# A Fourier mix and a two-layer product on one core: an opening with another stage A and other weight order, and a chunk's block sums moved behind other work

## The chip, the cores and the metric

The kernel runs on one core of a Trainium2 chip. The time is that of the device for one execution, in microseconds (us). Five engines work beside each other and wait for each other through semaphores: TensorE (PE) multiplies matrices into PSUM, VectorE (DVE), ScalarE (ACT) and GpSimd (POOL) work on elements, and SyncE (SP) issues the transfers, which 16 DMA engines carry out between the device memory and the on-chip buffers.

## The reference

```python
# x: (8, 3008, 256); w_r, w_i: (256, 256); b_r, b_i: (256,)
X = np.fft.rfft(x, axis=1)                      # along the 3008 positions
Yr = Xr @ w_r - Xi @ w_i + b_r
Yi = Xr @ w_i + Xi @ w_r + b_i
Y  = sign(Y) * max(|Y| - 0.01, 0)               # for Yr and Yi each
y  = np.fft.irfft(Y, n=3008, axis=1)            # float32
# y as (24064, 256); w_in: (256, 2048); w_out: (2048, 256), both float64
h  = np.maximum(y @ w_in, 0.0)
out = (h * h @ w_out).astype(np.float32)
```

## The kernel before, in words

3008 = 47 x 64, and the transform is done in two factors. Position n is written with n1 (47 values) and n2 (64 values); of the 47 frequencies of the first factor only r = 0 to 23 are needed, since x is real.

- **Stage A** is the 47-point transform. The host has paired the rows n1 and 47 - n1 (`folded_rows`), 24 pairs for each n2, and lays five n2 side by side, so a tile has 120 rows (`GROUPS`: 12 of width 5 and one of 4, 96 rows). VectorE adds and subtracts the two halves (`fold`, L214 and L215), and two products with the table `tA` give `psa`. ScalarE copies it (`eva`) and a transfer stores it in a scratch area in device memory, `scr1[r, n2, ...]`, 24 outer rows (`store_a`, L207).
- **Stage B** goes over 12 pairs of frequencies r. Per pair it loads 128 rows (`bin`, `load_b`), does the 64-point transform (`points_b`, L223, tile `psb`), mixes with w_r and w_i (three real products instead of four, with the sum of both parts `sum_x` and with combined weights; `psm`), adds the bias (`add_e`), takes the threshold, turns the result (`zh`), does the 64-point inverse (`psc`) and stores `evc` in a second scratch area (`store_c`, L211).
- **The inverse** of the first factor loads 120 rows of it for five n2 (`din`, L251), multiplies (`points_d`, `psd`, L261), and unfolds (`dx`), and the result `xt`, split into a high and a low part, is the input of the second half. Two such groups, 470 positions, are a chunk; there are 52.
- **The two-layer product** takes a chunk in 8 rounds. In a round `mm1` makes 256 of the 2048 hidden rows (12 matmuls of 470 columns, `ph`), `squares` and `sums` make seven combinations `g` of them, which are split into `gh` and `gl`, and `mm2`, two rounds later, does 21 matmuls with the prepared weights `wo_` into four accumulators `po`. Products are exact to float32 by three matmuls with high and low parts (`mm3`, L186 to L188). When a chunk's last round is done, `put_together` makes the output from the four accumulators: a ScalarE copy and seven VectorE sums (L768 to L776).

The opening, `start()`, does stage A and stage B of batch 0, stage A of batch 1, the first chunk's inverse, and brings w_in and w_out in: they come as float64, 512 KB a piece, and `narrow` makes float32 of the bits. In the opening the products of stages A and B are plain float32 matmuls, and the order of instructions on the engines is left to a scheduler. The batches after that do the same stages inside the main rounds, on a plan written out by hand: `plan_a`, `plan_b` and `plan_d` put each step at a round and a place, and a round runs its places in this order: load, a1, `mm1`, p1, `squares`, v1, `sums`, `mm2`, p2, a2, `put_together` if a chunk ends here, v2. The letter says the engine: a ScalarE, v VectorE, p TensorE.

At v2 stand the low part of a stage A input (`fl`, L557), that of a stage B input (`xl`, L606), the adding of the bias and the unfolding `dx`; what uses them stands mostly in p1 of the next round. The small products take their PSUM from two buffers (`ps_f`) in turn.

Of the kernel before, what the change touches and what calls it, by code (L numbers as in the profile page):

```python
# [44 lines left out]
W = 5  # L45
# [34 lines left out]

def _cs(num, den):

    num = np.asarray(num) % den
    ang = 2.0 * np.pi * num / den
    c, s = np.cos(ang), np.sin(ang)
    c = np.where((4 * num) % (2 * den) == den, 0.0, c)
    s = np.where((2 * num) % den == 0, 0.0, s)
    return c, s


def tables():
# [39 lines left out]
    return dict(t_a=ta.astype(np.float32), t_b=tb.astype(np.float32), t_m=tm.astype(np.float32),  # L131
# [15 lines left out]
def fft_mix_moe(ctx: ExitStack, tc: tile.TileContext, xp, w_r, w_i, b_r, b_i,  # L147
                w_in, w_out, t_a, t_b, t_m, t_d, sgn, outT):
    nc = tc.nc
    B = xp.shape[0]  # L150
# [24 lines left out]
    wi_ = [ctile(f"wi{k}", [P, 2, DFF], F32R) for k in range(2)]  # L175
    wo_ = []

    def split(src, hi, lo):

        nc.scalar.copy(hi, src)  # L180
        nc.vector.tensor_sub(lo, src, hi.bitcast(F32))
# [16 lines left out]
    def load_x(b, i, t):  # L198
        nc.sync.dma_start(out=t, in_=xp[b].rearrange("g p d -> p g d")[:t.shape[0], i, :])
# [76 lines left out]
    def start():  # L276

        with ExitStack() as own:
            sb = own.enter_context(tc.tile_pool(name="sb0", bufs=2))
            pp = own.enter_context(tc.tile_pool(name="ps0", bufs=8, space=bass.MemoryType.PSUM))  # L280

            def tl(tag, shape=(P, 512), dt=F32, bufs=2, name=None):
                return sb.tile(list(shape), dt, tag=tag, name=name or tag, bufs=bufs)
# [4 lines left out]
            tA = tl("tA", (120, 4, 120), bufs=1)  # L288
            tM = tl("tM", (P, P), bufs=1)
            wmf = [tl(f"wmf{k}", (P, 3, D), bufs=1) for k in range(2)]  # L290

            def load_mix():
                nc.sync.dma_start(out=tB[:, :5], in_=t_b[:, :5])
                yield
                wr = tl("ld", bufs=4, name="wr").rearrange("p (k e) -> p k e", k=2)
                wi = tl("ld", bufs=4, name="wi").rearrange("p (k e) -> p k e", k=2)
                nc.sync.dma_start(out=wr, in_=w_r.rearrange("(k p) e -> p k e", p=P))
                nc.sync.dma_start(out=wi, in_=w_i.rearrange("(k p) e -> p k e", p=P))
                nc.sync.dma_start(out=bias2[:, 0, :], in_=b_r.partition_broadcast(P))
                nc.sync.dma_start(out=bias2[:, 1, :], in_=b_i.partition_broadcast(P))  # L300
                nc.sync.dma_start(out=sg, in_=sgn)
                nc.sync.dma_start(out=tM, in_=t_m)
                yield
                for k in range(2):
                    nc.scalar.copy(wmf[k][:, 0], wr[:, k])
                    nc.vector.scalar_tensor_tensor(wmf[k][:, 1], wr[:, k], -1.0, wi[:, k],
                                                   op0=ALU.mult, op1=ALU.subtract)
                    nc.vector.tensor_sub(wmf[k][:, 2], wi[:, k], wr[:, k])
                nc.sync.dma_start(out=tB[:, 5:], in_=t_b[:, 5:])
                nc.sync.dma_start(out=tD, in_=t_d)  # L310
                yield

            def narrow(t, h):
# [4 lines left out]
                nc.scalar.activation(h, hi.bitcast(F32), AF.Abs)  # L318
                nc.vector.tensor_scalar(h, h, F_MIN, F_MAX, op0=ALU.max, op1=ALU.min)
# [7 lines left out]
            def load_w(src, use):  # L327

                h = tl("w32")
                if src.dtype == F32:  # L330
                    nc.sync.dma_start(
                        out=h.rearrange("p (f n) -> p f n", f=2) if len(src.shape) == 3 else h, in_=src)
                    yield
                else:
                    t = tl("w64", (P, 512, 2), U32)
# [6 lines left out]
                    narrow(t, h)  # L342
                use(h)

            def load_win():
                for c in range(DFF // 512):
                    for k in range(2):
                        s = slice(512 * c, 512 * c + 512)

                        def use(h, k=k, s=s):  # L350
                            split(h, wi_[0][:, k, s], wi_[1][:, k, s])

                        yield load_w(w_in[k * P:(k + 1) * P, s], use)

            def load_wout():
                wo_.extend(ctile(f"wo{k}", [P, NU, NPR, P], F32R) for k in range(2))
                wv = w_out.rearrange("(f p) e -> p f e", p=P)
                for j in range(NU):
                    def use(h, j=j):
                        a = h.rearrange("p (f e m) -> p f e m", f=2, e=2)  # L360
                        w7 = tl("w7", (P, NPR, P), bufs=1)
                        nc.scalar.copy(w7[:, 0:3:2], a[:, :, 0])
                        nc.scalar.copy(w7[:, 1], a[:, 1, 1])
                        nc.vector.tensor_add(w7[:, 4], a[:, 0, 1], a[:, 1, 1])
                        nc.vector.tensor_sub(w7[:, 6], w7[:, 4], a[:, 0, 0])
                        nc.vector.tensor_sub(w7[:, 5], a[:, 0, 0], a[:, 0, 1])
                        nc.vector.tensor_sub(w7[:, 3], a[:, 1, 0], w7[:, 6])
                        split(w7, wo_[0][:, j], wo_[1][:, j])

                    yield load_w(wv[:, 2 * j:2 * j + 2, :], use)  # L370

            def rolling(pieces):

                last = None
                for p in pieces:
                    next(p)
                    if last is not None:
                        for _ in last:
                            pass
                        yield  # L380
                    last = p
                for _ in last:
                    pass
                yield

            def stage_a(b):
                scratch1(b)
                if b == 0:
                    st = [const.tile([P, 8, 512], F32, tag=f"wo{k}", name=f"x0{k}") for k in range(2)]
                    xv = xp[b].rearrange("g p d -> p g d")  # L390
                    for g0, g1 in ((0, 1), (1, 2), (2, 4), (4, 6), (6, 8), (8, 10), (10, 12), (12, 13)):
                        n = NR * GROUPS[g0][1]
                        k = g0 // 8
                        nc.sync.dma_start(out=st[k][:n, g0 - 8 * k:g1 - 8 * k, :], in_=xv[:n, g0:g1, :])
                    yield
                for i, (g, w) in enumerate(GROUPS):
                    n = NR * w
                    tab = 0 if w == W else 2
                    if b == 0:
                        t = st[i // 8][:n, i % 8, :]  # L400
                    else:
                        t = tl("ld", bufs=4, name="xin")[:n]
                        load_x(b, i, t)
                    f = tl("f")[:n]
                    fold(f, t)
                    o = pst("psa")[:n]
                    for c in range(2):
                        cs = slice(c * D, c * D + D)
                        nc.tensor.matmul(o[:, cs], tA[:n, tab + c, :n], f[:, cs], start=True, stop=True)
                    e = tl("ev", bufs=4, name="eva")[:n]  # L410
                    nc.scalar.copy(e, o)
                    store_a(b, i, e)
                    yield

            def stages_b():
                scratch2(0)
                xs, zs, got = {}, {}, {}

                def load(i):
                    got[i] = tl("ld", bufs=4, name="bin")  # L420
                    load_b(0, i, got[i])

                load(0)
                load(1)
                for i in range(NPAIR + 2):
                    if i + 2 < NPAIR:
                        load(i + 2)
                    if i < NPAIR:
                        ps = pst("psb")
                        points_b(ps, i, got.pop(i))  # L430
                        x = xs[i] = tl("x", (P, 3, 2, P))
                        take_b(x, ps)
                        sum_x(x)
                        yield i
                    if 0 <= i - 1 < NPAIR:
                        x = xs.pop(i - 1)
                        p = pst("psm1"), pst("psm2")
                        for comp, mat, bank, half in MIX:
                            for k in range(2):
                                nc.tensor.matmul(p[bank][:, half * D:half * D + D], x[:, comp, k],  # L440
# [414 lines left out]
```

## Time and profile before

| | |
|---|---|
| median of 3 runs (lowest, highest) | 2755.3 us (2751.26 to 2757.68) |
| the profiled execution | 2757.75 us |
| its span, first to last instruction | 2756.0 us |
| TensorE busy | 2621.9 us, 95% of the span |
| VectorE, ScalarE busy | 2160.0 us (78%), 2050.9 us (74%) |
| GpSimd busy | 0.2 us |
| moved by transfers | 163.94 MB, mean 59 GB/s |
| first matmul of the main rounds | 164.41 us after the span's start |

Matmuls are pipelined, and a matmul's end in the profile is modelled, so how many microseconds TensorE is idle says more than its busy share. PEclk is the TensorE clock that was granted, as a share of full speed; the DMA share is the mean over the 16 DMA engines of the time that their packets took. In lists of instructions the columns are start and duration in us, engine (with a q: its queue of issues), line, operation, what is written from what, and in brackets the idle time before it and what ended it. In a list of waits: who waited for whom, then us in total, how many times, the longest.

### The profile page before, as it was taken

What the parts mean: (1) busy time and instruction counts of PE and PEld (TensorE: products, weight loads), DVE (VectorE), ACT (ScalarE), POOL (GpSimd) and SP (SyncE); (2) the same over time, 40 slices, a digit from 0 to 9 for tenths busy, and PEclk for the clock granted to TensorE, in tenths of its full rate; (3) what the DMA queues carried; (4) which work ended last, traced back from release to release, by engine and by line L of the source; (5) the groups of instructions that cost most, each with busy time, mean ns of one, the idle gap of its engine ahead of it and who ended that gap; (6) DMA issues with size and microseconds to landing.
All of it is one profiled execution on the core that took longest, in us unless ns stands there. A gap on an engine that the chain in (4) does not pass through costs nothing.

```text
span 2756.0 us, 45108 instructions
## 1 busy us (share of the span) xinstructions
PE 2621.9 (95%) x17832; PEld 2443.3 (89%) x17832; DVE 2160.0 (78%) x3383; ACT 2050.9 (74%) x2917; POOL 0.2 (0%) x4
## 2 busy tenths in 40 slices
PE   5679999999999999999999999999999999999998
PEld 4469999999889999999999999899989999999998
DVE  5858888788877888878887888778888888777776
ACT  4757778678777778777777777777777777766665
POOL 0000000000000000000000000000000000000000
PEclk8789999999999999999999999999999999999999
DMA  7431113111121112311122111311113111000000
GB/s 218 141 103 34 52 45 96 53 49 44 57 90 41 54 44 68 93 37 53 41 89 70 38 46 48 95 52 51 46 59 100 42 36 55 26 28 24 19 26 18
DMA packets 128245, 163.94 MB, mean 59 GB/s; under 512 B 10931, under 2 KB 87971, under 8 KB 128035
## 3 DMA queue, kind: packets, MB, share of 16 engines
q1 hardware_dynamic: 128035, 161.06, 19.5%
q8 instruction: 142, 2.33, 0.4%
q14 instruction: 68, 0.56, 0.1%
HBM read 86.04 MB, written 74.97 MB: 58 GB/s over the span
## 4 chain that ended last, share of the span: by engine, by line
PE 65%; DVE 15%; ACT 14%; issue 3%; DMA 3%; SPq 0%; ACTq 0%; DVEq 0%
PE ph L186 9%; PE ph L187 9%; PE ph L188 8%; PE po L188 8%; PE po L187 8%; PE po L186 8%; ACT gh L793 6%; DVE gl L801 3%; PE psd L261 2%; PE psb L223 2%; ACT g L743 2%; DVE g L750 2%; ACT g L744 2%; PE psm L188 2%; PE psm L186 2%
## 5 line engine op out<-in xcount | busy, mean ns | idle before, releaser
L801 DVE TENSOR_TENSOR gl<-g,gh 128x1652 fp32r<-128x1652 f32 (+1 forms) x416 | 770.4, 1852 | 384.1 <-ACT gh L793 384.1
L793 ACT CAST gh<-g 128x1652 fp32r<-128x1652 f32 (+1 forms) x416 | 645.7, 1552 | 438.7 <-DVE g L752 241.8
L186 PE MATMUL po<-gh,wo 128*128 128x236 f32 (+1 forms) x2912 | 811.6, 279 | 2.2 <-DVE o L775 1.4
L187 PE MATMUL po<-gl,wo 128*128 128x236 f32 (+1 forms) x2912 | 803.8, 276 | 2.4 <-DVE gl L801 2.4
L188 PE MATMUL po<-gh,wo 128*128 128x236 f32 (+1 forms) x2912 | 805.0, 276 | 0.0
L186 PE MATMUL ph<-xt,wi 128*128 128x470 f32 (+1 forms) x1664 | 634.0, 381 | 6.1 <-ACT g L743 5.3
L187 PE MATMUL ph<-xt,wi 128*128 128x470 f32 (+1 forms) x1664 | 623.7, 375 | 3.8 <-DVE xt L697 3.8
L188 PE MATMUL ph<-xt,wi 128*128 128x470 f32 (+1 forms) x1664 | 619.0, 372 | 0.0
L186 PEld LDWEIGHTS po<-gh,wo 128*128 128x128 f32 x2912 | 559.9, 192 | 10.3 <-DVE o L775 2.7
L187 PEld LDWEIGHTS po<-gl,wo 128*128 128x128 f32 x2912 | 559.5, 192 | 7.7 <-DVE gl L801 2.8
L188 PEld LDWEIGHTS po<-gh,wo 128*128 128x128 f32 x2912 | 561.3, 193 | 0.0
L743 ACT ACTIVATE g<-ph 128x472 f32<-128x472 f32 (+1 forms) x832 | 417.4, 554 | 105.0 <-PE ph L188 100.3
L744 ACT ACTIVATE g<-g 128x944 f32<-128x944 f32 (+1 forms) x416 | 408.8, 983 | 13.2
L186 PEld LDWEIGHTS ph<-xt,wi 128*128 128x128 f32 x1664 | 316.1, 190 | 40.0 <-ACT g L743 8.6
L188 PEld LDWEIGHTS ph<-xt,wi 128*128 128x128 f32 x1664 | 314.5, 189 | 39.0
L187 PEld LDWEIGHTS ph<-xt,wi 128*128 128x128 f32 x1664 | 317.0, 190 | 33.0 <-DVE xt L697 6.1
L750 DVE TENSOR_TENSOR g<-g 128x472 f32<-128x472 f32 (+1 forms) x416 | 266.7, 641 | 41.5 <-ACT g L744 28.0
L752 DVE TENSOR_TENSOR g<-g 128x236 f32<-128x236 f32 (+1 forms) x416 | 166.5, 400 | 14.4
L751 DVE TENSOR_TENSOR g<-g 128x236 f32<-128x236 f32 (+1 forms) x416 | 166.5, 400 | 14.3
L188 PE MATMUL psm<-wm,xl 128*128 128x256 f32 x504 | 142.2, 282 | 15.4 <-DVE xl L606 15.4
L186 PE MATMUL psm<-wm,xh 128*128 128x256 f32 x504 | 140.0, 278 | 0.0
L187 PE MATMUL psm<-wm,xh 128*128 128x256 f32 x504 | 139.9, 277 | 0.0
(97 smaller groups left out, 2797.4 us busy)
## 6 DMA issues: line engine op xcount, KB each, us to landing
bin<-s SPq DMA_DIRECT2D x96, 256.0 KB
s<-evc SPq DMA_DIRECT2D x96, 256.0 KB
s<-eva SPq DMA_DIRECT2D x96, 240.0 KB
din<-s SPq DMA_DIRECT2D x96, 240.0 KB
xin<-in_xp_dram SPq DMA_DIRECT2D x84, 240.0 KB
outT_dram<-o SPq DMA_DIRECT2D x96, 118.0 KB
outT_dram<-o SPq DMA_DIRECT2D x96, 117.0 KB
w<-in_moe_w_in_dram SPq DMA_DIRECT2D x8, 512.0 KB
```

Of the source, the lines that this page charges most:

```text
L186: nc.tensor.matmul(out, l0, r0, start=start, stop=False, **kw)
L187: nc.tensor.matmul(out, l0, r1, start=False, stop=False, **kw)
L188: nc.tensor.matmul(out, l1, r0, start=False, stop=stop, **kw)
L223: nc.tensor.matmul(ps[:, k, :, q, :], tv[:, q, k], tB[:, 0:r + 2:r + 1], start=True, stop=True)
L261: nc.tensor.matmul(ps[:, k, part], t[:n, s:s + P], tD[:n, tab + part, :n], start=True, stop=True)
L743: nc.scalar.activation(g[:, t:4:2, :m], ph[:, :, t * t0:t * t0 + m], AF.Relu)
L744: nc.scalar.activation(g[:, 0:4, :m], g[:, 0:4, :m], AF.Square)
L750: nc.vector.tensor_sub(g[:, 4:6, :m], g[:, 1:4:2, :m], g[:, 0:2, :m])
L751: nc.vector.tensor_sub(g[:, 6, :m], g[:, 3, :m], g[:, 4, :m])
L752: nc.vector.tensor_sub(g[:, 1, :m], g[:, 6, :m], g[:, 2, :m])
L793: nc.scalar.copy(gg[k][0][:, :, :m], hid[k][:, :, :m])
L801: nc.vector.tensor_sub(gg[k][1][:, :, :m], hid.pop(k)[:, :, :m], gg[k][0][:, :, :m].bitcast(F32))
```

## The change

- **Stage A of batches 0 and 1** no longer folds. The host passes x of these two batches as `xu`, with the 94 rows (n1, parity of n2) and 32 columns of n2, each of 256 numbers. A table `tU` of 94 x 96 gives both parts of the 24 frequencies in one float32 matmul of 512 columns for two neighbours of each parity; there are 16 of them in place of 13 pairs. The 96 result rows are (parity, part, r), and each half is stored on its own: 4 outer rows of 24 in `scr1`. x of batch 0 is loaded at the start, in seven transfers, into the place of `wi_`; x of batch 1 comes in 16 transfers, two in each step of the pair loop, into the place of `wo_`, which becomes eight tiles for each part.
- **The mix** of batch 0 uses four real products with high and low parts in place of three float32 ones, with the bias as one more row, so that `sum_x` and `add_e` go there. The combined weights for the later batches are made near the end of the opening.
- **Weights**: each piece is loaded two calls before its bits are worked on, with four buffers, and its work is spread over the following calls. Subtractions and sums of weights move to GpSimd.
- **The order** in the opening is now written out by hand. Steps of stage A of batch 1 stand in each step of the pair loop from the third on.
- **In the main rounds** the matmuls of stage A move from p1 to p2 and the copy of their result to a1 of the round after (but for the last group). `put_together` stands behind v2.

```diff
+def plain_rows():
+    n2 = np.arange(N2).reshape(-1, 2)
+    return ((64 * np.arange(N1)[:, None, None] + 47 * n2.T[None]) % S).reshape(2 * N1, N2 // 2)
...
-    wi_ = [ctile(f"wi{k}", [P, 2, DFF], F32R) for k in range(2)]
-    wo_ = []
+    wi_ = []
+    wo_ = [], []
...
-        nc.sync.dma_start(out=t, in_=xp[b].rearrange("g p d -> p g d")[:t.shape[0], i, :])
+        nc.sync.dma_start(out=t, in_=xp[b - NPLAIN].rearrange("g p d -> p g d")[:t.shape[0], i, :])
...
+            x0 = [const.tile([P, nq, D], F32, tag=f"wi{k}", name=f"x0{k}") for k in range(2)]
+            def load_x0(k, parts):
+                for g0, g1 in parts:
+                    nc.sync.dma_start(out=x0[k][:2 * N1, g0:g1, :], in_=xu[0, :, nq * k + g0:nq * k + g1, :])
+            def load_x1():
+                i = len(x1)
+                if i < nq:
+                    x1.append(const.tile([P, 2, D], F32, tag=f"wo{i % 2}{i // 2}", name=f"x1{i}"))
+                    nc.sync.dma_start(out=x1[i][:2 * N1], in_=xu[1, :, 2 * i:2 * i + 2, :])
...
+            def loads():
+                dma = nc.sync.dma_start
+                dma(out=tU, in_=t_u)
+                load_x0(0, ((0, 2), (2, 4), (4, 8), (8, 12), (12, 16)))
+                for k in range(2):
+                    dma(out=raw[k][:, 1], in_=w_r[k * P:k * P + P, :])
+                    dma(out=raw[k][:, 2], in_=w_i[k * P:k * P + P, :])
+                load_x0(1, ((0, 8), (8, 16)))
...
+            def weights(begin=True):
+                for p in list(going):
+                    if next(p, going) is going:
+                        going.remove(p)
+                p = next(pending, None) if begin else None
+                if p is not None:
+                    next(p)
+                    going.append(p)
+                return bool(going)
...
             def stage_a(b):
-                    f = tl("f")[:n]
-                    fold(f, t)
-                    o = pst("psa")[:n]
-                    for c in range(2):
-                        cs = slice(c * D, c * D + D)
-                        nc.tensor.matmul(o[:, cs], tA[:n, tab + c, :n], f[:, cs], start=True, stop=True)
-                    e = tl("ev", bufs=4, name="eva")[:n]
-                    nc.scalar.copy(e, o)
-                    store_a(b, i, e)
+                v = scr1[b].rearrange("r n (c d) -> (n c) r d", c=2)
+                for i in range(nq):
+                    t = x1[i][:2 * N1] if b else x0[i // 8][:2 * N1, 2 * (i % 8):2 * (i % 8) + 2, :]
+                    o = pst("psa")[:4 * NR]
+                    nc.tensor.matmul(o, tU, t.rearrange("p k d -> p (k d)"), start=True, stop=True)
+                    e = tl("ev", bufs=3, name="eva")[:4 * NR]
+                    copy(i, e, o)
+                    for k in range(2):
+                        q = 8 * i + 4 * k
+                        nc.sync.dma_start(out=v[q:q + 4], in_=e[:, k * D:k * D + D])
...
+            def pair_mix(i):
+                h, l = xs.pop(i)
+                p = pm[i] = pst("psm")
+                for n in range(2):
+                    nc.tensor.matmul(p, one, rows[n], start=n == 0, stop=False)
+                for c in range(2):
+                    for k in range(2):
+                        w = slice(D - D * c, 3 * D - D * c)
+                        mm3(p, (h[:, k, c], l[:, k, c]), (w3[0][:, k, w], w3[1][:, k, w]),
+                            False, c + k == 2)
...
+            loads()
+            a0, a1 = stage_a(0), stage_a(1)
+            for i, _ in enumerate(a0):
...
+            for i in range(3):
+                load_pair(i)
+            more_loads()
+            weights()
...
+            for n in range(NPAIR + 3):
+                load_pair(n + 3)
+                load_x1()
+                load_x1()
+                if 0 <= n - 2 < NPAIR:
+                    pair_z(n - 2)
+                if n < NPAIR:
+                    pair_b(n)
+                if 0 <= n - 1 < NPAIR:
+                    pair_mix(n - 1)
+                if n >= 3:
+                    pair_c(n - 3)
+                    pair_out(n - 3)
+                if n >= 2:
+                    next(a1)
+                if 0 <= n - 2 < NPAIR:
+                    pair_turn(n - 2)
...
+                weights()
+            inv = inverse(0, xt)
...
-                at(r + 1, "p1", points)
-                at(r + 1, "a2", out)
+                at(r + 1, "p2", points)
+                at(*((r + 2, "a1") if i + 1 < len(GROUPS) else (r + 1, "a2")), out)
...
             run(r, "p2")
             run(r, "a2")
+            run(r, "v2")
             if k >= 0 and jj == NU - 1:
                 put_together(cc, pos.pop(cc))
-            run(r, "v2")
...
+    xu = x[:2, plain_rows()]
+    xp = np.zeros((nb - 2, len(GROUPS), NR * W, 2, D), x.dtype)
```

More of the change, by code (lines that the diff above doesn't have):

```diff
@@ L286, in pst @@
                 return pp.tile([P, 512], F32, tag="f", name=name)
[L288 to L296, printed above, removed]
+            tM = tl("tM", (P, P))
@@ new lines, in loads @@
+            def loads():
[6 more added lines that the diff above has]
+                load_x0(1, ((0, 8), (8, 16)))
+                dma(out=row[:, :D], in_=b_r[None, :])
+                dma(out=row[:, D:], in_=b_i[None, :])
+                nc.vector.memset(ones, 1.0)
+                nc.scalar.copy(one, ones)
@@ L341, in load_w @@
                     yield
[L342 to L346, printed above, removed]
-                    for k in range(2):
[L348 to L370, printed above, removed]
@@ L372, in rolling @@
-            def rolling(pieces):
-                last = None
-                for p in pieces:
-                    next(p)
[L377 to L384, printed above, removed]
+                    yield
+                    h = tl("w32", bufs=3)
+                    yield from narrow(t, h)
+                yield
@@ new lines, in weight, with win, use @@
+                yield from use(h)
+            def win(c, k):
+                def use(h):
+                    if not wi_:
+                        wi_.extend(ctile(f"wi{k}", [P, 2, DFF], F32R) for k in range(2))
+                    s = slice(512 * c, 512 * c + 512)
+                    nc.scalar.copy(wi_[0][:, k, s], h)
+                    yield
+                    nc.gpsimd.tensor_sub(wi_[1][:, k, s], h, wi_[0][:, k, s].bitcast(F32))
+                return weight(w_in[k * P:(k + 1) * P, 512 * c:512 * c + 512], use)
@@ L386, in stage_a, with copy @@
+            def copy(n, out, in_):
+                (nc.vector.tensor_copy if n % 2 else nc.scalar.copy)(out, in_)
             def stage_a(b):
                 scratch1(b)
[L388 to L394, printed above, removed]
-                    yield
@@ new lines, in pair_turn, with pair_c @@
+            def pair_turn(i):
+                z = zs[i].rearrange("p (c e) -> p c e", c=2)
+                zh = zs[i] = tl("zh", (P, 2, D), bufs=2)
+                for q in range(2):
+                    r = 2 * i + q
+                    src = slice(64 * q, 64 * q + 64)
+                    nc.vector.tensor_copy(zh[:64, q], z[src, 0])
+                    nc.scalar.activation(zh[64:, q], z[src, 1], AF.Copy, scale=sg[src, 1, r:r + 1])
+            def pair_c(i):
+                pc[i] = pst("psc")
+                nc.tensor.matmul(pc[i], tM, zs.pop(i).rearrange("p q e -> p (q e)"), start=True, stop=True)
@@ new lines, in start @@
+            late = tables_main()
+            for n in range(NPAIR + 3):
[15 more added lines that the diff above has]
+                    pair_turn(n - 2)
+                if n == NPAIR - 2:
+                    nc.sync.dma_start(out=tD, in_=t_d)
+                    next(late)
+                if n == NPAIR + 1:
+                    next(late, None)
+                weights()
@@ L492, in start @@
             inv = inverse(0, xt)
             next(inv)
[L494 removed]
+            next(a1, None)
+            weights()
+            for _ in inv:
                 next(a1, None)
[L496 to L505 removed]
+                weights()
@@ L506, in start @@
+            for _ in a1:
+                weights()
+            while weights():
+                pass
             return xt
```

215 lines of the change are left out of this document (109 added, 106 removed).

## The prediction

> **What bounds the kernel now.** I read the page first, then the busy time by stage, the waits, and at last the order of time at single places.
>
> ```profile
> span 2756.0 us, 45108 instructions
> PE   5679999999999999999999999999999999999998
> DMA  7431113111121112311122111311113111000000
> ```
> The page: TensorE is nearly full from the fourth slice on, where the DMA engines are almost idle. The first two slices and a half are the opening, and there it is the other way round.
>
> ```profile
> core 0: us, PE busy (x) PEld busy (x) DVE busy (x) ACT busy (x) POOL busy (x), PEclk, DMA share, GB/s
> 0.00:32.90 32.90, 14.42 (x52) 9.88 (x52) 10.07 (x28) 9.47 (x15) 0.20 (x4) 0.89 0.80 218
> 32.90:132.90 100.00, 70.88 (x275) 52.71 (x276) 82.84 (x173) 71.95 (x139) 0.00 (x0) 0.81 0.55 169
> 132.90:164.40 31.50, 17.41 (x59) 12.75 (x57) 10.34 (x26) 8.29 (x15) 0.00 (x0) 0.64 0.58 170
> 164.40:2756.00 2591.60, 2519.22 (x17448) 2367.94 (x17448) 2056.75 (x3156) 1961.21 (x2748) 0.00 (x0) 0.99 0.17 52
> ```
> By stage: stage A of batch 0 takes 32.9 us and moves 218 GB/s; the pairs of stage B take 100 us for 14 steps, 7.1 us a step; the inverse of the first chunk and the rest of stage A of batch 1 take 31.5 us; the main rounds begin at 164.4 us. No stage of the opening is full on one engine, and the first is nearest to it on the DMA engines.
>
> ```profile
> PE psa L187 <- DVE fl L557: 17.2, 13, 2.6
> PE psm L188 <- DVE xl L606: 15.4, 13, 2.1
> PE psc L186 <- DVE dx L269: 10.9, 8, 1.5
> PE psd L261 <- ACT evc L648: 7.5, 4, 2.3
> PE ph L186 <- ACT g L743: 5.3, 5, 2.3
> PE ph L187 <- DVE xt L697: 3.8, 8, 0.6
> PE po L186 <- DVE o L775: 1.4, 7, 0.2
> ```
> Waits of TensorE in the main rounds (us in total, times, longest): the three largest, 43.5 us, are all for work of place v2.
>
> **The change part by part.** *Closing sums behind v2, stage A's points at p2.* At one chunk's close:
> ```profile
> 1003.41 0.39 DVE L776 TENSOR_TENSOR o<-o,po 128x236 f32<-128x236 f32 x1
> 1003.71 0.95 DVE L606 TENSOR_TENSOR xl<-x,xh 128x768 fp32r<-128x768 f32 x1
> 1004.72 0.19 PEld L188 LDWEIGHTS psm<-wm,xl 128*128 128x128 f32 x1 [1.54 <-DVE xl L606]
> ```
> xl stands behind the last of the seven block sums, and TensorE waits for it. In the new order xl comes first and that wait goes; likewise dx, and fl, whose matmuls also move behind the second product. The psd waits come where psa stands ahead in p1, so they go with the move: 17.2 + 15.4 + 10.9 + 7.5 = 51.0 us. Against it the sums end 0.7 to 1.4 us later; what then comes late is the bank that the next chunk's product overwrites (1.4 us today, 0.2 at most each). If every one of the 34 mended closings lost 1 us there, 17 us would be left. The first bank is read by the first two sums only, so I take a loss of 6: gain 45 us, bounds 17 and 51. The psa copy moved to the next round's a1 is one ScalarE copy, hidden since ScalarE is busy 1961 of 2592 us; if not, TensorE's next first product waits as in the 5.3 us row.
>
> *No folding, no sums of x, no added bias.* VectorE loses 52 folds in the opening:
> ```profile
> L214 DVE TENSOR_TENSOR f<-x 120x256 f32<-120x256 f32 x12 | 5.1, 423 | 8.9 <-DMA x<-in_xp_dram 8.2 <-PE psa L409 0.7
> ```
> At 0.42 us they are 22 us, yet they waited for the load (8.2 us), so I cost them at nothing on the path; the same holds for the sums and the bias, which lie beside the transfers. GpSimd takes over the low parts of the weights and the sums of w_out:
> ```profile
> L181 DVE TENSOR_TENSOR wo<-w,wo 128x896 fp32r<-128x896 f32 x8 | 8.7, 1085 | 0.1
> L181 DVE TENSOR_TENSOR wi<-w,wi 128x512 fp32r<-128x512 f32 x8 | 5.5, 688 | 0.4 <-ACT wi L180 0.3
> ```
> No row shows GpSimd arithmetic. At VectorE's pace it is under 30 us in all, at three times that under 90, spread over the opening, and the last weights are first read some rounds into the main part: nothing between these ends, unless the opening were shorter than 90 us.
>
> *TensorE in the pair steps.*
> ```profile
> 1000.64 0.37 PE L187 MATMUL ph<-xt,wi 128*128 128x470 f32 x1
> 1000.85 0.37 PE L188 MATMUL ph<-xt,wi 128*128 128x470 f32 x1
> 77.44 1.05 PE L223 MATMUL psb<-tB,bin 128*128 128x128 f32 x8
> 76.47 1.12 PE L456 MATMUL psc<-zh,tM 128*128 128x512 f32 x2 [0.17 <-ACT zh L452]
> ```
> 470 columns follow each other after 0.21 us, so 512 take 0.23, and the mix of 14 such takes 3.2 us; with psb (1.05), psc (1.0) and a stage A matmul of the psc form (1.0) a step is 6.3 us, 6.4 with a little waiting, against 7.1.
>
> *The transfers.* This decides. Three stretches with one kind of transfer each, or nearly:
> ```profile
> 5.20:7.70 2.50, 2.50 (x6) 1.97 (x7) 1.60 (x4) 0.42 (x1) 0.00 (x0) 1.00 0.98 232
> 21.50:26.50 5.00, 0.00 (x0) 0.00 (x0) 0.00 (x0) 2.34 (x4) 0.00 (x0) 0.91 0.71 225
> 37.50:40.50 3.00, 2.99 (x14) 3.00 (x15) 0.79 (x3) 0.59 (x1) 0.00 (x0) 0.50 1.01 360
> ```
> Loads of x (120 rows) and of tables and weights (128 rows) fill the engines: share 0.98 and 1.01. The stores of stage A go from 120 rows into 24 outer rows, and though stores are always waiting, the share is 0.71. Twelve of 16 is 0.75, and 12 is the largest count up to 16 that divides both 24 and 120. I therefore read: a transfer is dealt out in equal pieces over a count of engines that divides the outermost length of both sides. The changed kernel loads x of batches 0 and 1 from and into 94 = 2 x 47 rows, so over two engines, and stores each half of a stage A result as 4 outer rows of 24, so over four. Both lots meet on the same two engines if a small count always takes the first ones; that is my reading too.
>
> On the rule itself, from the Trainium skill, page "DMA: Bandwidth & Descriptors", section "Why a DMA increments its semaphore by 16 and not by 1": a copy on the hardware path uses the largest k up to 16 that divides the slowest dimension of both patterns, on the lowest-numbered engines. By that rule the loads here have k = 2 and the stores k = 4, and the time is the sum below; without it, the first rival's. The 0.71 agrees with its k = 12; no run here shows a k below 12.
>
> One engine's pace: 360 GB/s over 16 is 22.5 GB/s (21.50:26.50 gives 225/12 = 18.8, 5.20:7.70 gives 232/15 = 15.5). I take 22.5, since with two engines at work little contends. The queue is served in order:
> ```profile
> 1.25 4.68 SPq L394 DMA_DIRECT2D x<-in_xp_dram  x8
> 7.89 20.88 SPq L207 DMA_DIRECT2D s<-eva  x13
> 19.26 0.58 ACT L411 COPY eva<-psa 120x512 f32<-120x512 f32 x1 [7.56 <-PE psa L409]
> 132.87 0.37 SPq L211 DMA_DIRECT2D s<-evc  x1
> 135.56 0.78 SPq L251 DMA_DIRECT2D din<-s  x1
> ```
> All loads of x are issued by 5.9 us; the first store, issued at 7.9, has not given its buffer back until about 19.3, when the loads are done (four buffers; the fifth copy waits, and TensorE had long been done). So stores queue behind loads.
>
> Load on each of the two engines, in order. *Stage A of batch 0:* start 2 us and the table 0.8; x 94 x 32 KB = 3.08 MB, half on each, 68.5 us; mix weights, two weight pieces and a table 5; 32 stores of 96 KB, a quarter each, 35 us; landing 1.5. Sum 113 us against 32.9. Its pairs cannot start before, since the first bin load needs all of them. *Steps 0 to 7:* per step two x loads of batch 1 (8.6 us), one bin (0.73) and one weight piece (1.46), from step 2 two stores of stage A (2.2), from step 3 one evc store (0.73): 86 + 13.1 + 3.6, and 5.5 for the first bins and tables, 108 us; TensorE's 6.4 us a step lies under it. Now 221 us. The bins and weights go over all engines, as these rows' sizes and 128 rows say:
> ```profile
> bin<-s SPq DMA_DIRECT2D x96, 256.0 KB
> w<-in_moe_w_in_dram SPq DMA_DIRECT2D x8, 512.0 KB
> ```
> but an eighth of nothing helps: each lands only when its share behind the x loads does. *Steps 8 to 14:* the two engines need 5.1 us, so TensorE's 6.4 sets the pace, 45 us: 266. *Inverse of chunk 0:* the last evc store lands 2.7 us after its issue (132.87 to 135.56), the din load as much again, then
> ```profile
> 150.94 1.05 PE L261 MATMUL psd<-tD,din 120*128 120x120 f32 x8
> 154.60 1.39 DVE L181 TENSOR_TENSOR xt<-dx,xt 128x470 fp32r<-128x470 f32 x2
> ```
> 5.1 us from the first psd to the last xt: 10.5, taken as 11. The main rounds begin at 277 us, 113 later than now.
>
> **Sum.** The profiled execution took 2757.75 us, 1.75 over its span and 2.5 above the median of 2755.3. 2757.75 + 113 - 45 = 2826 us.
>
> **The rivals.** *The loads go over all engines* (faster). If 94 rows are split in another way, x arrives as now, stage A takes its 32 us, 15 steps of 6.2 us make 93, the rest of stage A is inside them and the tail is 12: main rounds at 137, 27 earlier; 2757.75 - 27 - 45 = 2686. For it: the rows show only counts from 12 to 16. Against it: 120 rows into 24 were not split in another way either. It decides from about four engines for the loads: then the 137 us that x of both batches takes on the busiest engine halve, the opening's loss of 113 falls to some 45, and the main rounds' gain makes it even. *Only the loads are narrow:* the stores go over 16; 30 us off stage A, 13 off the steps: 2783. *The closing sums come late instead:* VectorE, already at 2057 of 2592 us, passes the wait to the next product; gain near nothing: 2871 at most, 2854 with the 17.
>
> **How the numbers follow.** Narrow loads and stores with the main rounds' gain 0.75, with the gain lost 0.08; narrow loads only 0.05; all engines 0.12. The likeliest gives 2826. Its own range: at 24.5 GB/s the 185 us that x and the stores take on the busiest engine fall by 15, and with the full 51 in the main rounds that is 2805; at the stores' 18.8 they grow by 36, and with some of the gain lost it is 2885. The range reaches down to 2778 to take in the case of narrow loads only. All engines (0.12) and the slow ends of the lost gain stay outside. A measurement of this kernel tells about 0.2%, 5.5 us. Slower 0.85, within 0.03, faster 0.12.
>
> **What would show it.** After: x loads landing over about 68 us, a DMA share near 0.13 while they run alone; TensorE near idle until 110 us; first main product at 250 to 300 us; the waits on fl, xl and dx nearly gone, the wait on the block sums a few us. If the share is near 1 at 3 to 16 us and the first main product stands before 150, the reading of 94 rows is wrong and the kernel is faster.

## The result, and the profile after

The changed kernel takes 2825.0 us (median of 4 runs, 2823.24 to 2826.25) where the kernel before takes 2755.8 (median of 4 as well): slower by a ratio of 1.0253 [1.0235, 1.0271], 69 us. Its profiled execution took 2825.74 us, its span 2823.9. The page of the changed kernel, its span, TensorE's line and the DMA engines' line of the 40 slices:

```profile
span 2823.9 us, 45012 instructions
...
PE   3556999999999999999999999999999999999998
...
DMA  1443111221113111221113111221113111000000
```

The opening now fills nearly four slices of 70 us, and the DMA engines, which stood at 7 tenths in the first slice, stand at 1. The busy time by stage of the changed kernel (us, busy time of TensorE, weight loads, VectorE, ScalarE and GpSimd, granted clock, DMA share, GB/s):

```profile
3.00:8.00 5.00, 0.00 (x0) 0.00 (x0) 0.00 (x0) 0.00 (x0) 0.00 (x0) 1.00 0.13 48
45.00:66.00 21.00, 5.40 (x6) 1.52 (x6) 0.00 (x0) 0.00 (x0) 0.00 (x0) 1.00 0.16 62
75.00:86.00 11.00, 3.23 (x4) 0.39 (x2) 4.39 (x6) 3.98 (x7) 0.00 (x0) 1.00 0.27 96
0.00:100.78 100.78, 30.60 (x32) 7.17 (x32) 8.03 (x13) 9.70 (x16) 0.20 (x4) 1.00 0.22 79
250.00:268.18 18.18, 7.55 (x21) 4.32 (x21) 16.03 (x16) 8.39 (x17) 17.66 (x18) 0.50 0.20 61
268.18:2823.90 2555.72, 2516.02 (x17448) 2362.59 (x17448) 2054.12 (x3156) 1958.51 (x2748) 1.20 (x1) 1.00 0.18 52
```

While only x is loaded, the share is 0.13, two engines of 16, and 48 GB/s; while stage A's results are stored, 0.27 and 96 GB/s, about four engines. Stage A of batch 0 ends at 100.8 us (32.9 before), and the main rounds begin at 268.2 us (164.4 before), 103.8 later. They take 2555.7 us where they took 2591.6, 35.9 less. 103.8 - 35.9 = 67.9 us is the difference of the spans. The waits of TensorE in the main rounds of the changed kernel (us in total, times, longest), the answers to the seven rows of before and one more for the block sums:

```profile
PE ph L200 <- ACT g L829: 8.1, 8, 2.4
PE ph L201 <- DVE xt L783: 3.9, 8, 0.6
...
PE psm L202 <- DVE xl L692: 3.6, 11, 0.9
PE psa L200 <- ACT evc L734: 3.6, 1, 3.6
PE psc L200 <- DVE dx L283: 2.8, 7, 0.9
PE psd L275 <- DVE dx L283: 2.5, 6, 0.5
...
PE po L200 <- DVE o L861: 1.7, 9, 0.2
PE po L200 <- DVE o L856: 1.5, 3, 0.7
```

The 17.2 us for `fl` are gone, `xl` fell from 15.4 to 3.6 and `dx` in front of psc from 10.9 to 2.8. The block sums (`o`) rose from 1.4 to 1.7 us in this row, and a second row of theirs, 1.5 us, came new; nothing large is late in their place.

The order of transfers that SP issued in the opening of the changed kernel (start, duration, line, transfer):

```profile
0.74 0.37 SPq L331 DMA_DIRECT2D tU<-in_t_u_dram  x1
1.17 7.78 SPq L316 DMA_DIRECT2D x<-in_xu_dram  x5
...
14.12 8.25 SPq L335 DMA_DIRECT2D raw<-in_w_i_dram  x1
...
31.93 9.28 SPq L337 DMA_DIRECT2D row<-in_b_r_dram  x1
41.26 1.20 SPq L338 DMA_DIRECT2D row<-in_b_i_dram  x1
42.58 26.67 SPq L472 DMA_DIRECT2D s<-eva  x8
```

A single issue of 1 KB (`row`) held SP for 9.28 us, the next, of as much, for 1.20. So the narrow loads do not only land late, they keep the queue's issuer from its next transfers: the first store of stage A is issued at 42.6 us. With x loaded over all engines (96 rows, the first experiment below) the two issues of `row` take 0.23 us each and the first store is issued at 12.0. The stores then queue behind x, as the prediction read it: ScalarE's and VectorE's copies wait until 67.3 us and later for the buffers of stores issued from 42.6 us on, and x, 3.08 MB at 48 GB/s, needs about 64 us.

### The profile page after: what moved, and what is told of

It reads as the page before. It is cut to its first block, busy times and chain, and to the rows that moved or that the text cites. A ratio compares the mean times of both kernels' runs of the same rounds, so it can differ in the third digit from the quotient of the medians.

```text
span 2823.9 us, 45012 instructions
## 1 busy us (share of the span) xinstructions
PE 2652.5 (94%) x17816; PEld 2434.8 (86%) x17816; DVE 2145.0 (76%) x3301; ACT 2031.8 (72%) x2885; POOL 52.6 (2%) x60
## 4 chain that ended last, share of the span: by engine, by line
PE 44%; DVE 23%; ACT 18%; issue 5%; DMA 1%; ACTq 0%; DVEq 0%; SPq 0%
ACT gh L879 9%; DVE gl L887 6%; PE ph L200 6%; PE ph L201 6%; PE ph L202 6%; PE po L202 6%; PE po L201 6%; PE po L200 5%; DVE g L836 4%; ACT g L830 3%; ACT g L829 3%; DVE g L837 3%; DVE g L838 2%; PE psm L202 2%; PE psb L237 2%
## 5 line engine op out<-in xcount | busy, mean ns | idle before, releaser
L202 PE MATMUL psm<-wm,xl 128*128 128x256 f32 (+1 forms) x552 | 162.1, 294 | 3.6 <-DVE xl L692 3.6
L200 PE MATMUL psm<-wm,xh 128*128 128x256 f32 (+1 forms) x552 | 161.4, 292 | 0.0
L201 PE MATMUL psm<-wm,xh 128*128 128x256 f32 (+1 forms) x552 | 159.6, 289 | 0.0
```

What stands on the lines that cost most here:

```text
L200: nc.tensor.matmul(out, l0, r0, start=start, stop=False, **kw)
L201: nc.tensor.matmul(out, l0, r1, start=False, stop=False, **kw)
L202: nc.tensor.matmul(out, l1, r0, start=False, stop=stop, **kw)
```

## The experiments

The theory after the first comparison: the opening's loss comes from the number of DMA engines that a transfer gets, and the main rounds' gain from the block sums' place. The first rival for the opening was that its own work (a longer mix, GpSimd, another order) is slower; for the main rounds, that moving stage A's matmuls to p2 brings a good part. All kernels but two start from the changed kernel.

**Loads of 96 rows.** The host appends two rows of zeros to x's 94.

```diff
-                    nc.sync.dma_start(out=x0[k][:2 * N1, g0:g1, :], in_=xu[0, :, nq * k + g0:nq * k + g1, :])
+                    nc.sync.dma_start(out=x0[k][:96, g0:g1, :], in_=xu[0, :, nq * k + g0:nq * k + g1, :])
...
-                    nc.sync.dma_start(out=x1[i][:2 * N1], in_=xu[1, :, 2 * i:2 * i + 2, :])
+                    nc.sync.dma_start(out=x1[i][:96], in_=xu[1, :, 2 * i:2 * i + 2, :])
...
+    xu = np.pad(xu, ((0, 0), (0, 96 - 2 * N1), (0, 0), (0, 0)))
```

> Theory (a transfer runs over the largest count of DMA engines up to 16 that divides the outermost length of both sides): two empty rows are added to x of batches 0 and 1, so its loads go over 16 engines instead of 2, while the stores of stage A stay on 4. Stage A of batch 0 then hangs on its stores, 3.15 MB at the 97 GB/s that they showed, 32 us, and ends at about 46 us instead of 101; the pair steps run at TensorE's pace, about 6.6 us each, and the main rounds begin at about 172 us instead of 268: 2729 us. Rival (x is slow because its rows lie 32 KB apart, whatever their count): still about 2825 us, DMA share 0.13 while x loads.

Measured: 2730.35 us, 0.9903 [0.9885, 0.992] of the kernel before; main rounds from 171.9 us, 2553.2 long. The same five microseconds as above, in this kernel:

```profile
3.00:8.00 5.00, 3.28 (x4) 1.24 (x5) 0.00 (x0) 0.58 (x1) 0.00 (x0) 1.00 0.91 249
```

0.91 instead of 0.13, 249 GB/s instead of 48, with two more rows to move. The opening is 96.3 us shorter by this alone.

**Stores of 24 outer rows.** The table's columns are put in another order, so that a store runs over r first.

```diff
-    tu = np.zeros((N1, 2, 2, 2, NR))
+    tu = np.zeros((N1, 2, NR, 2, 2))
...
-                v = scr1[b].rearrange("r n (c d) -> (n c) r d", c=2)
+                v = scr1[b].rearrange("r n (c d) -> r (n c) d", c=2)
...
-                        nc.sync.dma_start(out=v[q:q + 4], in_=e[:, k * D:k * D + D])
+                        nc.sync.dma_start(out=v[:, q:q + 4], in_=e[:, k * D:k * D + D])
```

> Theory: only the stores of stage A are widened (the table's columns in another order, so that 24 outer rows are stored: 12 engines by the rule instead of 4), the loads of x stay on 2. x of batch 0 still needs about 62 us, its stores end some 12 us later, the first eight pair steps still wait for x of batch 1 at 10 to 11 us each; main rounds at about 240 us instead of 268: 2797 us. If stores and loads had not met on the same two engines, the stores would have hidden beside the loads and the change would be near nothing in the pair steps: 2815 us or more.

Measured: 2810.63 us, 1.0196 [1.0177, 1.0215]; main rounds from 250.8 us. The stores' stretch of this kernel:

```profile
72.00:86.00 14.00, 3.18 (x4) 0.52 (x2) 4.84 (x7) 5.48 (x10) 0.00 (x0) 1.00 0.53 150
```

The share rises from 0.27 to 0.53, so the stores are wider than four engines; that they get twelve (0.75) this share does not show. The time lies between the two that were expected, 13.6 us above the theory's and nearer to the other: the main rounds come 17.4 us earlier, 9.7 of them in stage A, which ends at 91.1 us, and 7.7 in the pair steps. Stage A still waits for its loads, and its stores then take 25 us and not 12; what they hang on is shown with the last experiment. Behind wide loads the same edit brings less still:

**Both.** The two edits above together.

```diff
+    xu = np.pad(xu, ((0, 0), (0, 96 - 2 * N1), (0, 0), (0, 0)))
...
+                v = scr1[b].rearrange("r n (c d) -> r (n c) d", c=2)
```

> Theory: loads of x over 16 engines and stores over 12. Stage A of batch 0 ends at about 30 us, 15 pair steps at 6.6 us, a tail of 20 to 27 us: main rounds at about 152 us, 2708 us. The rival that the new opening is slow for another reason than the transfers (TensorE's four products, GpSimd's slow share, the order by hand) expects the main rounds at 200 us or later and more than 2755 us.

Measured: 2722.29 us, 0.9871 [0.985, 0.9891]; main rounds from 165.3 us, 6.6 earlier than with wide loads alone. With both, 268.2 - 165.3 = 102.9 of the opening's 103.8 us are gone: the widths of the transfers are the whole loss against the old opening. But 14 us of what was expected didn't come: stage A ends at 45.6 us, where the old, folding one ended at 32.9, and the new opening is as long as the old one (164.4).

**Loads of 95 rows**, to see whether the count follows the divisor and not just "few" or "many": 95 is 5 x 19. Against the kernel with 96 rows; the two loads likewise take `:95`.

```diff
-    xu = np.pad(xu, ((0, 0), (0, 96 - 2 * N1), (0, 0), (0, 0)))
+    xu = np.pad(xu, ((0, 0), (0, 95 - 2 * N1), (0, 0), (0, 0)))
```

> As the kernel with 96 rows, but with one empty row only: 95 = 5 x 19. Theory (largest count up to 16 that divides both lengths): the loads of x go over 5 engines; x of batch 0 lands in about 26 us, the DMA share while it loads alone is 0.31, its stores end at about 65 us, a pair step needs 8 us on the busiest engine, main rounds at about 190 us: 2749 us. If the count only had to be even, or the engines were taken by blocks of rows, 95 rows would be like 94 (2825 us) or like 96 (2730 us).

Measured: 2754.85 us, 0.9997 [0.9986, 1.0007]; main rounds from 196.4 us. Its stretch of x loads:

```profile
10.00:28.00 18.00, 14.15 (x17) 4.48 (x18) 0.00 (x0) 0.58 (x1) 0.00 (x0) 1.00 0.32 128
```

Five of 16 engines are 0.31; 0.32 was measured, and 128 GB/s, 25.6 an engine. The two rivals, 2825 and 2730 us, are out. One row of zeros is worth 70 us, the second another 24.5.

**The old opening with the two moves of the main rounds.** From the kernel before.

```diff
-                at(r + 1, "p1", points)
-                at(r + 1, "a2", out)
+                at(r + 1, "p2", points)
+                at(*((r + 2, "a1") if i + 1 < len(GROUPS) else (r + 1, "a2")), out)
...
+            run(r, "v2")
             if k >= 0 and jj == NU - 1:
                 put_together(cc, pos.pop(cc))
-            run(r, "v2")
```

> The opening of the kernel before with the changed kernel's main rounds only (block sums behind v2, stage A's matmuls at p2). Theory: the main rounds gained 36 us by the trace (2591.6 to 2555.7 us), and all of it comes from these two moves: 2720 us. Rival (part of it comes from the opening having finished more by then, or from other state that it leaves): 2735 us or more.

Measured: 2717.31 us, 0.9855 [0.984, 0.9871]; main rounds from 163.2 us, 2553.0 long. The main rounds' gain, 38.6 us here, needs nothing of the new opening.

**The block sums ahead of v2 again**, with stage A's matmuls left at p2.

```diff
-            run(r, "v2")
             if k >= 0 and jj == NU - 1:
                 put_together(cc, pos.pop(cc))
+            run(r, "v2")
```

> The changed kernel with the block sums again ahead of v2; stage A's matmuls stay at p2. Theory: only the waits on xl and dx come back (12 and 8 us by the difference of the two traces), the one on fl does not, since its matmuls stand late: 2845 us. Rival (the order of the sums is the whole gain): 2861 us.

Measured: 2851.51 us, 1.0352 [1.0331, 1.0374]; main rounds 2580.1 us, 24.4 longer than in the changed kernel. TensorE's waits in its main rounds:

```profile
PE psm L202 <- DVE xl L692: 16.1, 13, 2.2
PE psc L200 <- DVE dx L283: 11.3, 9, 1.4
```

Both waits are back at what they were before (15.4 and 10.9). The `fl` wait is not, since its matmuls stand behind the second product. The time lies between theory and rival: with the waits for `g`, 11.2 us against 8.1 in the changed kernel, the three rows have grown by 24.1 us. Against the kernel before, whose sums also stand ahead, the main rounds are 11.5 us shorter (2591.6 to 2580.1): as long as the sums are in the way, the move to p2 pays by itself, as far as two kernels with different openings tell.

**Stage A's matmuls at p1 again**, with the sums left behind v2.

```diff
-                at(r + 1, "p2", points)
-                at(*((r + 2, "a1") if i + 1 < len(GROUPS) else (r + 1, "a2")), out)
+                at(r + 1, "p1", points)
+                at(r + 1, "a2", out)
```

> The changed kernel with stage A's matmuls back at p1 and the copy back at a2; block sums stay behind v2. Theory: the wait of psd behind psa (7 us) comes back, and a few us of the wait on fl in rounds without a close: 2835 us. Rival (the move to p2 does nothing, the sums did it all): 2825 us.

Measured: 2825.71 us, 1.0255 [1.0235, 1.0275]; main rounds 2554.7 us. The theory's 2835 was wrong, the rival's 2825 right. TensorE's waits in its main rounds:

```profile
PE psd L275 <- ACT evc L734: 8.0, 4, 2.3
PE psa L201 <- DVE fl L643: 5.4, 11, 0.9
...
PE ph L200 <- ACT g L829: 2.8, 4, 1.2
```

The waits of psd are back in full and `fl` in part, 13.4 us together, and the main rounds are not longer. The wait for `fl` was mostly the block sums' too (17.2 before, 5.4 here). And what the move to p2 takes away is paid elsewhere: for `g` it is 2.8 us here and 8.1 in the changed kernel, and the 3.6 for `evc` and the 2.5 for `dx` in front of psd, which stand among the changed kernel's rows, are not among this one's: 11.4 us of the 13.4. Some 2 us of the difference for `g` lie in the first 12 us of the main rounds, next to the opening, so these rows don't match one for one. As a whole TensorE is idle for 37.8 us of the main rounds here (2554.7 less 2516.9 busy) and for 39.7 in the changed kernel (2555.7 less 2516.0). The move exchanges waits.

**The one line alone, in the kernel before.** The same swap of `put_together` and v2 as the second part of the old opening's edit, and nothing else.

```diff
+            run(r, "v2")
             if k >= 0 and jj == NU - 1:
                 put_together(cc, pos.pop(cc))
-            run(r, "v2")
```

> The kernel before with one line moved: `put_together` stands behind v2; stage A's matmuls stay in p1 and the copy of their result in a2. Theory (this line carries the whole gain of the main rounds, and moving stage A's matmuls adds nothing): main part 2553 to 2558 us, median 2718, ratio 0.986, as the old opening with both moves (2717). Rival (the move to p2 is needed for the waits of psd on evc, 7.5 us in the kernel before, which then remain in full and are not taken from another wait): 2725, ratio 0.989. Second rival (what the sums ahead of v2 cost with the matmuls at p2, 26 us, is all that the line is worth): 2730, ratio 0.991.

Measured: 2715.62 us, 0.9862 [0.9842, 0.9883]. Its stage view from the first main product on, and its waits there:

```profile
163.00:2713.70 2550.70, 2512.30 (x17448) 2360.85 (x17448) 2053.13 (x3156) 1957.12 (x2748) 0.00 (x0) 1.00 0.18 53
```
```profile
PE psd L261 <- ACT evc L648: 8.3, 4, 2.3
PE psa L187 <- DVE fl L557: 4.9, 9, 0.9
PE ph L186 <- ACT g L743: 4.5, 4, 2.3
...
PE psm L188 <- DVE xl L606: 3.5, 11, 0.9
PE psc L186 <- DVE dx L269: 2.6, 7, 1.1
```

The main rounds are 40.9 us shorter than before (2591.6 to 2550.7), the most of any kernel here, while the 8.3 us for `evc` stay; both rivals are out. This line alone gives all of the change's gain in the main rounds.

**No work on GpSimd.** The kernel with both widths, with every operation of GpSimd on VectorE.

```diff
-                    nc.gpsimd.tensor_sub(wi_[1][:, k, s], h, wi_[0][:, k, s].bitcast(F32))
+                    nc.vector.tensor_sub(wi_[1][:, k, s], h, wi_[0][:, k, s].bitcast(F32))
...
```

> The kernel with both transfers widened, and all of GpSimd's arithmetic in the opening put on VectorE. Theory: after the last pair, ScalarE waits for GpSimd's sums of weights, the eva copy stands behind that and the din load behind its store; and VectorE's own instructions run up to 3.5 times as long while GpSimd works. Without GpSimd the tail from the last evc store to the main rounds falls from 26.5 us to about 14: 2711 us. Rival (VectorE, with 28 us more to do, becomes what the pair steps wait for): 2722 us or more.

Measured: 2716.36 us, 0.9857 [0.9833, 0.988]; main rounds from 159.9 us, 5.4 earlier than with GpSimd. The intervals of the two ratios overlap, so the difference in time rests on the trace. The end of the changed kernel's opening, in order of time:

```profile
241.65 0.38 SPq L225 DMA_DIRECT2D s<-evc  x1
...
246.56 2.06 POOL L438 TENSOR_TENSOR wo<-w,wo 128x896 fp32r<-128x896 f32 x1
248.65 0.41 ACT L427 COPY w<-w 128x256 f32<-128x256 f32 x1 [3.97 <-POOL wo L438]
...
249.72 0.56 ACT L458 COPY eva<-psa 96x512 f32<-96x512 f32 x1
...
250.31 1.24 SPq L472 DMA_DIRECT2D s<-eva  x2
...
250.62 2.25 POOL L438 TENSOR_TENSOR wo<-w,wo 128x896 fp32r<-128x896 f32 x1
...
250.97 2.45 DVE L385 SCALAR_TENSOR_TENSOR w<-w,w 128x512 uint32<-128x512 uint32 x1
251.72 0.81 SPq L265 DMA_DIRECT2D din<-s  x1
...
255.38 2.06 PE L275 MATMUL psd<-tD,din 120*128 120x120 f32 x8 [13.38 <-DMA din<-s]
...
260.63 2.09 POOL L438 TENSOR_TENSOR wo<-w,wo 128x896 fp32r<-128x896 f32 x1
...
260.81 2.41 DVE L195 TENSOR_TENSOR xt<-dx,xt 128x470 fp32r<-128x470 f32 x1 [0.65 <-ACT xt L194]
...
267.36 0.68 DVE L458 COPY eva<-psa 96x512 f32<-96x512 f32 x1
268.18 0.73 PE L200 MATMUL ph<-xt,wi 128*128 128x470 f32 x1 [3.72 <-DVE eva L458]
```

and two of the same instructions in the kernel without GpSimd:

```profile
146.72 0.69 DVE L385 SCALAR_TENSOR_TENSOR w<-w,w 128x512 uint32<-128x512 uint32 x1
...
154.44 0.65 DVE L195 TENSOR_TENSOR xt<-dx,xt 128x470 fp32r<-128x470 f32 x1 [0.65 <-ACT xt L194]
```

In the changed kernel a chain goes through three queues: ScalarE waits 3.97 us for GpSimd, the copy of stage A's result stands behind that, its stores at 250.31 stand behind the copy, and the load that the inverse needs stands behind the stores on SP, at 251.72, 10 us after the last `evc` store that it also needs. On VectorE the low part of `xt` takes 2.41 instead of 0.65 us. From the last `evc` store to the first main product it is 26.5 us in the changed kernel and in the one with both widths (138.79 to 165.33), and 16.1 without GpSimd (143.86 to 159.94); half of that gain is lost again, since the steps themselves end 5 us later with the work on VectorE, and the time is 5 us above the 2711 expected.

**The tables of the main rounds later.** The kernel with both widths; the arithmetic of `tables_main` is done behind the inverse.

```diff
-                if n == NPAIR + 1:
-                    next(late, None)
...
+            next(late, None)
```

> The kernel with both transfers widened and GpSimd as in the change; only the making of the later batches' tables moves from the last pair steps to behind the first chunk's inverse. Theory: in the tail the din load stands on SP behind a store whose copy stands on ScalarE behind work that waits for GpSimd; some 6 us of that work are these tables: 2716 us. Rival (they are covered, since the weights alone keep GpSimd full): 2722 us.

Measured: 2717.11 us, 0.9865 [0.9848, 0.9881]; main rounds from 154.8 us, 10.5 earlier, but 2561.6 long, 5.2 longer: the tables' work, taken out of the tail, delays the rounds behind it. The ratio is that of the kernel with both widths (0.9871) within their intervals, so no gain in time is shown, though the 2716 us were met.

**A shorter tail.** Without GpSimd, with late tables, stage A of batch 1 begun a step earlier, two weight pieces more in stage A of batch 0, and both `din` loads issued in the last step ahead of the stores.

```diff
-                if i in (11, 13):
+                if i in (9, 11, 13, 15):
...
+                if n == NPAIR + 2:
+                    inv = inverse(0, xt)
+                    next(inv)
-                if n >= 2:
+                if n >= 1:
```

> Both transfers widened, no GpSimd, the later tables behind the inverse, stage A of batch 1 one step earlier, weights begun one step earlier, both din loads issued right behind the last evc store. Theory: what is left of the opening is stage A (46 us), 15 pair steps at TensorE's 6.3 us, and a tail of 11 us and the last two steps of stage A: main rounds at about 148 us, 2703 us, below the old opening with the new main rounds (2717). Rival (the weights' work on VectorE and ScalarE only moves behind and holds up the first main rounds): 2712 us or more.

Measured: 2717.26 us, 0.9874 [0.9859, 0.989]; main rounds from 155.7 us, 2560.4 long. The rival was right about the time. Of the 14 us that were expected and didn't come, some 7.7 are the opening's own (155.7 instead of 148); and the main rounds are 5.6 us longer than without GpSimd alone (2554.8), for what leaves the tail stands in front of the first rounds. The first product of the next round waits there for the squares of ScalarE:

```profile
163.56 1.02 ACT L829 ACTIVATE g<-ph 128x472 f32<-128x472 f32 x2 [2.23 <-issue]
164.63 0.76 PE L200 MATMUL ph<-xt,wi 128*128 128x470 f32 x1 [4.55 <-ACT g L829]
```

**Four buffers.** The kernel with the shorter tail, with four buffers instead of three for the results of stage A and of the pairs, as the old stage A has for its own, against the copies' waits for stores.

```diff
-                    e = tl("ev", bufs=3, name="eva")[:4 * NR]
+                    e = tl("ev", bufs=4, name="eva")[:4 * NR]
...
-                ev = tl("ev", bufs=3, name="evc")
+                ev = tl("ev", bufs=4, name="evc")
```

> As the kernel before in this list, with four buffers in place of three for what stage A and the pairs store. Theory: stage A of batch 0 waits for its own stores to give buffers back (39 us of waits on stores and matmuls on VectorE); with four it ends about 7 us earlier: 2696 us. Rival (the store rate over 12 engines is the limit, 14 us for all, or the pace is the matmuls'): no change, 2703 us.

Measured: 2716.94 us, 0.9872 [0.9858, 0.9887]; stage A ends at 45.7 us, as with three. The copies' waits in its stage A of batch 0:

```profile
DVE eva L458 <- DMA s<-eva: 18.8, 6, 7.3
ACT eva L458 <- DMA s<-eva: 15.5, 5, 8.5
```

With three they were 15.9 and 18.1. One buffer more doesn't shorten it, so the theory fell. What the wide stage A hangs on up to 45.6 us, with a DMA share of 0.50 from 20 to 40 us, shows in SP's queue of the kernel with both widths:

```profile
22.49 12.88 SPq L472 DMA_DIRECT2D s<-eva  x16
...
147.46 1.52 SPq L472 DMA_DIRECT2D s<-eva  x2
```

From 22.49 us on SP issues one store after another, 0.8 us each, nearly as long as in the tail of the opening (1.52 for two), where the DMA share is 0.16 and none queue. 32 of them are 25 us of issuing, and 96 KB per 0.8 us are 123 GB/s, where the trace has 129 from 22.5 to 35.4 us. So neither buffers nor engines set the pace there, but SP's issue of the 32 stores. That is read from the trace; no run here made fewer and larger stores.

## Why the prediction was right, and where its terms were off

The direction, its cause and the time (2826 against 2825.0) came out as predicted. The sum is closer than its terms: the opening cost 103.8 us instead of 113, the main rounds gained 35.9 instead of 45, and the two errors cancel. That the time is met to within 1 us is luck.

- **The reading of 94 rows** held: shares 0.13 and 0.27 where 2 and 4 of 16 are 0.125 and 0.25, and 0.32 for 95 rows and 0.91 for 96. By the Trainium skill, page "DMA: Bandwidth & Descriptors", section "Why a DMA increments its semaphore by 16 and not by 1", 94, 95 and 96 rows get 2, 5 and 16 engines, as the largest counts up to 16 that divide them; these three traces agree. The two rivals with wide transfers (2686 and 2783) are out with it; the second had its term too large, since wide stores alone brought 14 us and not 43. The kernels that are wide show too what the first of them had mis-sized: its opening of 137 us was 165 (both widths), since stage A took 45.6 us and not 32, and the tail 26.5 and not 12.
- **The rate of an engine**, 22.5 GB/s by the sum, was 24 (48 over 2, 96 over 4); with 16 engines and 96 rows it was 15.6 (249 over 16), so eight times the engines brought five times the rate. Stage A ended at 100.8 instead of 113 and the steps, to the last `evc` store, took 140.9 us instead of 153. For 185 us on the busiest engine, 24 instead of 22.5 is 11.6 us of these 24. The seven steps that the sum put at TensorE's pace took 42.6 us instead of 45 (199.02 to 241.65 on SP), another 2.4. The rest wasn't split.
- **The inverse of chunk 0** was the term most off: 26.5 us instead of 11. The step that failed is "the din load as much again", right behind the last `evc` store: on SP it stood behind a store of stage A that waited for a copy that waited for GpSimd, and the two low parts of `xt` took 2.4 and 2.3 us. Shown by the tail above and by the kernel without GpSimd, whose 16.1 us leave 5 of the 15.5 to other causes, which were not separated.
- **GpSimd at nothing** was wrong in the same place. It was costed by its sum, 52.6 us busy as it turned out, well inside the bounds; what it cost was VectorE's time beside it and ScalarE's wait, some 5 us at the first main product.
- **The closing sums** held in kind: the waits for `fl`, `xl` and `dx` fell by 37 us, and the rival that the sums come late is out, with 3.2 us in their two rows. The 45 us counted the four waits as independent; 3.6 for `evc`, 3.6 for `xl` and 2.8 for `dx` stayed, and `dx` in front of psd (2.5) and `g` (2.8 more) came new. 51 - 10.0 - 5.3 = 35.7, against the 35.9 measured. Smaller rows are left out there, and it comes so near partly by chance: TensorE's idle time in the main rounds fell by 32.7 us (72.4 to 39.7), the rest of the 35.9 is its busy time, 2519.2 to 2516.0.
- **"The psd waits ... go with the move"** held as a wait and not as time: at p1 they are 8.0 us again in the main rounds, which take 2554.7 us against 2555.7. The move to p2 brings nothing beside the swap; the swap alone brings 40.9.

The change's opening, freed of its narrow transfers, is no better than the old one: 2722 and at best 2716 against 2715.6 for the old opening with the one line moved. That kernel is the one to keep: it is faster than the kernel before and the changed one, as fast within the intervals as the best of the others, and has the smallest edit.

## What to carry to other kernels

Before a tile is reshaped, look at the divisors of its row count: a DMA share of 0.13 while a queue was full meant two engines here, and two rows of zeros (94 to 96) made the opening 96 us shorter. In a queue, put what the bounding engine waits for ahead of what only closes an accumulation; one line moved was worth 38 us (0.9862 of 2753). Waits of the bounding engine that go away are no gain until the span shows it: 13.4 us of them came back here, and the main rounds were 1.0 us shorter.

## What the runs showed of the hardware that was not expected

- While two DMA engines had a backlog, SP's own issue was held: 8.25 and 9.28 us for one transfer of w_i or of 1 KB of bias, where others, of 1 KB and of the table `tU`, took 1.20 and 0.37. In the kernel with 96 rows the same two took 0.58 and 0.23. So a narrow transfer also delays those that go over all engines, by the issuer and not by the engines alone.
- VectorE's instructions with two inputs in SBUF took some 3.6 times as long beside GpSimd: 2.45 against 0.69 us and 2.41 against 0.65. At 250.97 and at 260.81 they end 0.55 and 0.50 us behind the end of the GpSimd instruction (252.87 and 262.72), which is little under their own time: they waited for all of it and then ran, as far as the rough ends of GpSimd's rows tell. By the Trainium skill, page "SBUF — State Buffer", section "Who interferes with whom", a VectorE instruction with two SBUF inputs and a GpSimd instruction that reads SBUF exclude each other, the later one waiting for the whole of the first; these rows agree.
- The issue of a store itself has a price on SP: with none queued, 0.76 us for the 24 outer rows of 4 (two in 1.52 with a DMA share of 0.16, both widths) and 0.62 for the 4 outer rows of 24 (two in 1.23 with a share of 0.03, the kernel with 96 rows), 96 KB each, where the 256 KB of `evc` took 0.38.
